# Reordering the turn from forward to backward in a one-core attention kernel: w3 before the rows of w4, q of the last head earlier, dq columns later

## The chip, the core and the metric

The kernel runs on one core of one Trainium2 chip. A core has a matrix engine (TensorE, PE in the profile), a vector engine (VectorE, DVE), an engine for functions of one element (ScalarE, ACT), GpSimd (POOL) and SyncE (SP), and 16 DMA engines that move data between HBM and the on-chip memories: SBUF, and PSUM, into which TensorE writes. Each engine takes its instructions in order. The metric is the device time of one execution in microseconds, as the median of several runs.

## The reference

One token passes through attention over a cache of 8192 keys and values in 32 heads of width 192, then through an MLP, both under adaptive layer norm. The reference returns the output and the gradients of nine inputs, the caches among them. Cut to what matters here (the mixer weights w1 and w2 and their inputs give no gradient that is returned, but w3 and w4 do):

```python
h = layernorm(x) * (1 + ca) + sa
q = (h @ wq).reshape(32, 192)
scores = einsum("hd,hkd->hk", q, k_cache) * 192 ** -0.5      # 8192 keys a head
o = einsum("hk,hkd->hd", softmax(scores), v_cache)
x = x + ga * (o.reshape(6144) @ wo)
h = layernorm(x) * (1 + cb) + sb
x1 = h                                                       # with one token the shifted mixer adds nothing
h2 = gelu(layernorm(x1) @ w3) @ w4                           # widths 640 -> 1536 -> 640
out = x + gb * (x1 + h2)
grads = vjp(out)(grad_out)       # d x, d k_cache, d v_cache, d wq, d wo, d w3, d w4, d c, d w_mod
```

The caches are 100 MB each and their gradients are as large, so the program reads and writes some 570 MB.

## The kernel before, in words

**Two loops and a turn between them.** The forward loop goes over heads 0 to 30 (`for i in range(H1)`). A head has K and V in two halves of 1536 KB, each 128 partitions by 32 keys by 192. For each head it forms the scores (VectorE products, summed by TensorE with the identity), the softmax, the weighted V (`vs`, four quarters a head, part on VectorE, part on ScalarE), and a matrix M = K^T (weighted V) with 193 columns, accumulated in the PSUM tile `mp` by `m_units`, from which dq is later made without reading K again. The backward loop goes over 64 half heads, last head first (`for s in range(NS)`): it reads a half of V, forms dP (products in `mul_q`, sums in `tree_q`, `dot_sum`), dS, the gradient of K (`dk_part`, VectorE: q times dS) and of V (`dv_groups`: TensorE outer products of a probability row and d(o), cast by ScalarE), and stores both through GpSimd's queue.

**The turn** lies between them and is a chain that nothing can be stored before: the last head's scores and output, the attention output, two layer norms, `n2_bf`, u = n2 @ w3 (`ups`, L831), gelu, d_g (eight or more calls in `dg_part`, VectorE sums of w4 rows times `dbo_bc`), du, dn = du @ w3^T (`dn_ps`, L926), and the gradient of the attention output `dao_bf` (L960). `w3t_gen` turns w3 by TensorE transposes in nine pieces, each copied out by ScalarE through two PSUM buffers; `w3t()` does the next piece. h2 = gelu(u) @ w4 (`h2_ps`) takes 60 matmuls of one column. `dw4_dve` and `dw4_act` form rows of the gradient of w4 in the place of the w4 rows in `qs_bc`. `do_mm(TL, b)` forms d(o) of one of the last two heads from `dao_bf`, and ScalarE writes it to `do_r`. After it come the first d(v) products, the trees of the first half head, and `q_bc(H1)`, which spreads the last head's q over the partitions for `dk_part`.

**What sets the order.** TensorE, VectorE, ScalarE and SyncE keep the order in which the program is written within each of two hand-ordered blocks (`manual_schedule`): the first ends with `d_sb_out`, the second begins after the backward pools are opened. Loads go on SyncE's queue in order: in the turn, the second half of V of the last head, w4 rows 0 to 3 with L660 into `w4b`, wo, rows 4 to 11 with L660 into `qs_bc` (called at L693), four fifths of w3 into `wp` (L695), the last fifth into `w3_4` (L704, named w in the profile), the V half for later (`v4`), the next wo, and the two probability rows `er_b` (L1002). A load is issued when its buffer is free: `wp` shares its buffer with the last score products. Stores go through GpSimd.

Pools of the forward part (`vs`, `ft`, the PSUM pools `psM`, `psO`, `psR`) end with the first block, and the backward pools (`bst` in SBUF, with `er_b`, `do_r`, `qh`; `psV`, `psR2`, `psT` in PSUM) take their space. `m_add` reads the tiles `mt` (pool `ft`) and `mp` (pool `psM`). For the last head q's dq has no M, so in half heads 0 and 1 `dq_rows` sums dS times K on TensorE and `dq_cols` turns the row into columns that VectorE adds.

The lines that wait for one another at the end of the first half heads, before the change:

```python
        if row is not None:
            dq_cols(row)
            row = None
        dk_part(dK, qh, dS4, 0, JQ)
```

Of the kernel before, what the change touches and what calls it, by code (L numbers as in the profile page):

```python
# [8 lines left out]
FP32 = mybir.dt.float32  # L9
# [11 lines left out]
def kernel(  # L21
# [27 lines left out]
    P = 128  # L49
# [55 lines left out]
    def pick(n, b):  # L105

        return ident_bf[0:n, b : b + 1].to_broadcast([n, P])
# [6 lines left out]
    def col(n, name, dtype=FP32):  # L114
        return const.tile([P, n], dtype, name=name)
# [5 lines left out]
    def mean_mm(src, n):  # L121
        ps = psS.tile([P, 32], FP32, name="mean_ps", tag="s")
        T_.matmul(ps[:, 0:n], lhsT=onesD, rhs=src, start=True, stop=True)
        return ps
# [235 lines left out]
    with tc.tile_pool(name="vs", bufs=3) as vsp, tc.tile_pool(name="ft", bufs=2) as ft, \  # L360
# [98 lines left out]
        def m_add(h, mp, mt):  # L459
            t, b = divmod(h, 2)  # L460
            V_.tensor_tensor(out=M2[64 * b : 64 * b + 64, t, :], in0=mp[0:64, MO : MO + MW], in1=mt[64:128, :], op=ALU.add)
# [49 lines left out]
        def dg_part(n):  # L511
            for a in dgs[:n]:
                V_.tensor_tensor_reduce(out=junk, in0=w4r(a), in1=dbo_bc, scale=1.0, scalar=0.0, op0=ALU.mult, op1=ALU.add, accum_out=d_g[:, a : a + 1])
            del dgs[:n]
# [3 lines left out]
        with tc.manual_schedule(engines=ORDER):  # L518
# [135 lines left out]
            def vs_act(vs, q, lo, hi):  # L654
                j0, v0 = q * JQ, (q % 2) * JQ
                for k in range(lo, hi):
                    A_.activation(out=vs[:, k, 0:DH], in_=vy[q // 2][:, v0 + k, :], func=ACT.Copy, scale=Ef[:, j0 + k : j0 + k + 1])

            def load_rows(dst, lo, hi):
                nc.sync.dma_start(out=dst.rearrange("p (a r) -> p a r", r=D), in_=w4v[:, lo:hi, :])  # L660
                for a in range(lo, hi):
                    w4rows[a] = dst[:, (a - lo) * D : (a - lo + 1) * D]
# [30 lines left out]
            load_rows(qs_bc[:, 0 : 8 * D], 4, 12)  # L693
# [10 lines left out]
            nc.sync.dma_start(out=w3_4, in_=w3d[:, 4, :])  # L704
            V_.tensor_copy(out=AO[:, :, 2 * TL - 2 : 2 * TL], in_=ps_ao)
# [37 lines left out]
            dg_part(1)  # L743
            V_.reciprocal(out=rinv[:, 2 * TL : 2 * TL + 2], in_=po[:, 4:6])
# [75 lines left out]
            def w3t(n=1):  # L820
                for _ in range(n):
                    next(w3t_it, None)

            w3t()
# [7 lines left out]
            m_add(H1 - 2, z["mp"], mt)  # L832
# [4 lines left out]
            vs_act(vs3, 3, 10, 14)  # L837
# [4 lines left out]
            A_.activation(out=w_, in_=w_, func=ACT.Exp, scale=-2.0 * GELU_K0)  # L842
            w3t()
# [12 lines left out]
            w3t()  # L856
            vs_act(vs3, 3, 14, JQ)
# [5 lines left out]
            pe.pop(0)()  # L863
            ps5 = mean_mm(sg.rearrange("p a b -> p (a b)"), 5 * ND)
# [20 lines left out]
            def dw4_dve(dst, a0, lo, hi):  # L885
                for a in range(lo, hi):
                    V_.tensor_scalar(out=dst[:, (a - a0) * D : (a - a0 + 1) * D], in0=dbo_bc, scalar1=g_[:, a : a + 1], scalar2=None, op0=ALU.mult)
# [25 lines left out]
            for k in range(ND):  # L913
                for a in range(NF):
                    T_.matmul(h2_ps[:, k : k + 1], lhsT=w4r(a)[:, k * P : (k + 1) * P], rhs=g_bf[:, a : a + 1], start=(a == 0), stop=(a == NF - 1))
# [12 lines left out]
            m_add(H1 - 1, mp, mt)  # L928
# [11 lines left out]
            V_.tensor_copy(out=bo, in_=h2_ps[:, 0:ND])  # L940
            dw4_dve(qs_bc, 0, 0, 3)
            pr = col(4 * ND, "pr").rearrange("p (a b) -> p a b", b=ND)
            V_.tensor_tensor(out=pr, in0=dn_ps[:, None, :].to_broadcast([P, 4, ND]), in1=G, op=ALU.mult)
            ps = mean_mm(pr.rearrange("p a b -> p (a b)"), 4 * ND)
# [5 lines left out]
            V_.scalar_tensor_tensor(out=B1, in0=vv, scalar=nr1, in1=dy_c, op0=ALU.mult, op1=ALU.add)  # L950
            d_n2, vg = col(ND, "d_n2"), col(ND, "vg")
            V_.tensor_tensor(out=vg, in0=Ag, in1=dn_ps, op=ALU.mult)
            V_.tensor_tensor(out=Bg, in0=B1, in1=ga, op=ALU.mult)
# [8 lines left out]
            dw4_dve(qs_bc, 0, 3, 6)  # L962
# [74 lines left out]

    do_mm(TL, 1)

# [36 lines left out]

    def q_bc(h):
        ps = psB.tile([P, 512], FP32, name="q_ps", tag="b")
        T_.matmul(ps[:, 0:DH], lhsT=pick(HQ, h), rhs=q_rows, start=True, stop=True)
        qh = bst.tile([P, DH], BF16, name="qh", bufs=2)  # L1080
        A_.copy(out=qh, in_=ps[:, 0:DH])
        return qh
# [241 lines left out]
    def dq_cols(row):  # L1324
        cp = psS.tile([P, 4], FP32, name="dq_c", tag="s")
        T_.matmul(cp[:, 0:1], lhsT=row[:, 0:P], rhs=c32[:, 0:1], start=True, stop=True)
        T_.matmul(cp[64:128, 1:2], lhsT=row[:, P:DH], rhs=c32[:, 0:1], start=True, stop=True)
        V_.tensor_tensor(out=dq_x[:, 2:3], in0=cp[:, 0:1], in1=dq_x[:, 2:3], op=ALU.add)
        V_.tensor_tensor(out=dq_x[64:128, 1:2], in0=cp[64:128, 1:2], in1=dq_x[64:128, 1:2], op=ALU.add)
# [44 lines left out]
    qh = q_bc(H1)  # L1374
    row = None
    late0 = [lambda: V_.scalar_tensor_tensor(out=du, in0=t_, scalar=-1.0, in1=d_g, op0=ALU.mult, op1=ALU.mult), dx1_out, d_sb_out]
    for s in range(NS):
# [47 lines left out]
        if row is not None:  # L1425
            dq_cols(row)
            row = None
# [10 lines left out]
        dk_store(s, dK, 0 if nxt else JQ, JH)  # L1438
        dv(5)
# [57 lines left out]
```

## Time and profile before

| | us |
|---|---|
| median of 3 runs | 1406.76 (1403.11 to 1409.83) |
| the profiled execution | 1405.93 |
| its span, first to last instruction | 1404.1 |
| TensorE busy | 1195.7 (85%) |
| VectorE busy | 1111.2 (79%) |
| ScalarE busy | 912.3 (65%) |
| transferred | 569.38 MB, mean 406 GB/s |

In the profile a line such as "L831" is a line of the kernel. "x60" counts instructions. A bracket at the end of a line of the timeline is the idle time of that engine before it and what ended it. The page cuts the span into 40 slices of 35.1 us; the granted clock of TensorE is given as a share of full speed. The times of the turn are counted in us from the start of the span.

### The profile page before, as it was taken

How to read it: one execution, taken by the hardware profiler on the slowest of the kernel's cores; microseconds unless marked ns; L12 is line 12 of the kernel's file. 1: busy time of each engine (PE TensorE's matmuls, PEld its weight loads, DVE VectorE, ACT ScalarE, POOL GpSimd, SP SyncE). 2: the span in 40 equal slices, each digit the busy share in tenths (PEclk: the TensorE clock that was granted, in tenths of full speed). 3: DMA queues.
4: the chain of work that ended last, by engine and by line, in shares of the span. 5: the costliest groups of instructions: out<-in, count | busy, mean ns of one | idle time of the engine just before them, and what ended most of it. 6: DMA issues, size and time to landing. Idle time of an engine off the chain costs nothing.

```text
span 1404.1 us, 30487 instructions
## 1 busy us (share of the span) xinstructions
PE 1195.7 (85%) x12712; PEld 748.7 (53%) x12712; DVE 1111.2 (79%) x1460; ACT 912.3 (65%) x2004; POOL 106.2 (8%) x192
## 2 busy tenths in 40 slices
PE   3999989999999998799866998698988987879985
PEld 2777777878777777543323444343443443334431
DVE  4999999999999997786765876776766767768775
ACT  0777777777777777566544766565656665556664
POOL 0000000000000000011110101101110101101110
PEclk9999999999999998755555555655555555555555
DMA  9999999999999997699999999999999999999998
GB/s 381 396 425 425 416 424 420 417 423 415 426 415 417 415 401 313 217 362 425 423 391 419 422 425 427 423 427 426 427 424 422 420 414 406 415 411 376 424 411 356
DMA packets 76232, 569.38 MB, mean 406 GB/s; under 512 B 7294, under 2 KB 25070, under 8 KB 36030
## 3 DMA queue, kind: packets, MB, share of 16 engines
q1 hardware_dynamic: 51146, 342.03, 59.5%
q0 software_dynamic: 24432, 224.89, 38.3%
q8 instruction: 99, 1.62, 0.4%
q10 hardware_dynamic: 516, 0.51, 0.1%
q14 instruction: 39, 0.32, 0.1%
HBM read 340.97 MB, written 226.44 MB: 404 GB/s over the span
## 4 chain that ended last, share of the span: by engine, by line
issue 48%; DVE 22%; DMA 11%; PE 9%; POOL 6%; ACT 2%; POOLq 0%; SPq 0%; ACTq 0%; DVEq 0%
DVE prod L333 9%; DMA KB<-in_A_k_cache_dram 8%; DVE prod L337 5%; DVE vs L383 3%; PE mp L405 3%; POOL out_dram L1337 2%; POOL out_dram L1333 2%; PE half_ps L343 2%; PE mp L410 1%; DMA out_dram<-VB 1%; DMA w<-in_B_w_dram 1%; DMA w_st<-in_A_wq_dram 1%; DVE pq L1044 1%; POOL out_dram L1176 1%; POOL out_dram L1203 1%
## 5 line engine op out<-in xcount | busy, mean ns | idle before, releaser
L1063 PE MATMUL dot_ps<-pq,ident_bf 128*128 128x256 bf16 x1494 | 384.4, 401 | 20.9 <-DVE dP L347 18.0
L390 ACT ACTIVATE vs<-VB,Ef 128x192 bf16<-128x192 bf16 x840 | 303.5, 447 | 0.0
L1075 ACT CAST KB<-dv_ps 128x768 bf16<-128x768 f32 x312 | 241.9, 803 | 78.2 <-PE dv_ps L1074 76.6
L1063 PEld LDWEIGHTS <-ident_bf 128*128 128x128 bf16 x1494 | 151.0, 124 | 178.6 <-issue 138.3
L1074 PE MATMUL dv_ps<-do_r,er_b 1*128 1x192 bf16 x2048 | 233.1, 341 | 3.0 <-ACT KB L1075 1.7
L333 DVE TENSOR_TENSOR prod<-KB,qs_bc 128x6144 bf16<-128x6144 bf16 x62 | 207.9, 3353 | 23.9 <-DMA KB<-in_A_k_cache_dram 16.2
L405 PE MATMUL mp<-vs,KB 128*128 128x193 bf16 x1984 | 190.2, 248 | 4.3 <-ACT vs L390 2.9
L1086 DVE TENSOR_TENSOR KB<-qh,dS 128x3072 bf16<-128x3072 bf16 x74 | 127.8, 1753 | 63.3 <-DMA out_dram<-KB 55.7
L405 PEld LDWEIGHTS <-KB 128*128 128x128 bf16 x1984 | 169.7, 98 | 13.4 <-DMA KB<-in_A_k_cache_dram 5.9
L902 ACT COPY wT<-wT_ps 128x1024 bf16<-128x1024 bf16 x82 | 79.1, 964 | 116.6 <-PE wT_ps L901 116.6
L1074 PEld LDWEIGHTS <-er_b 1*128 1x128 bf16 x2048 | 71.1, 105 | 148.7 <-issue 146.9
L343 PE MATMUL half_ps<-prod,ident_bf 128*128 128x256 bf16 x744 | 95.1, 279 | 43.2 <-DVE prod L337 43.1
L383 DVE TENSOR_TENSOR vs<-VB,E 128x1728 bf16<-128x1728 bf16 x120 | 123.7, 1052 | 0.3 <-ACT vs L390 0.3
L1044 DVE TENSOR_TENSOR pq<-VB,do_r 128x3072 bf16<-128x3072 bf16 x66 | 115.5, 1749 | 8.1 <-PE dot_ps L1063 8.1
L1044 DVE TENSOR_TENSOR pq<-KB,do_r 128x3072 bf16<-128x3072 bf16 x62 | 108.5, 1750 | 6.8 <-PE dot_ps L1063 6.2
L337 DVE TENSOR_TENSOR prod<-prod 128x3072 bf16<-128x3072 bf16 x62 | 108.7, 1754 | 1.0
L410 PE MATMUL mp<-vs,KB 128*64 128x193 bf16 x1976 | 107.5, 252 | 0.0
L343 PEld LDWEIGHTS <-ident_bf 128*128 128x128 bf16 x744 | 72.9, 99 | 61.5 <-issue 52.5
L1075 ACT CAST VB<-dv_ps 128x768 bf16<-128x768 f32 x96 | 75.1, 802 | 38.5 <-PE dv_ps L1074 38.3
L1075 ACT CAST qs_bc<-dv_ps 128x768 bf16<-128x768 f32 x104 | 80.6, 803 | 27.3 <-PE dv_ps L1074 26.9
L347 DVE TENSOR_REDUCE dP<-dot_ps 128x32 f32<-128x512 f32 x64 | 44.0, 688 | 62.6 <-PE dot_ps L1063 62.4
L410 PEld LDWEIGHTS <-KB 128*64 128x64 bf16 x1976 | 80.1, 110 | 19.9 <-issue 19.6
(369 smaller groups left out, 1191.7 us busy)
## 6 DMA issues: line engine op xcount, KB each, us to landing
VB<-in_A_v_cache_dram SPq DMA_DIRECT2D x93, 1536.0 KB
out_dram<-KB POOLq DMA_DIRECT2D x74, 1536.0 KB, 15.0
KB<-in_A_k_cache_dram SPq DMA_DIRECT2D x64, 1536.0 KB
KB<-in_A_v_cache_dram SPq DMA_DIRECT2D x31, 1536.0 KB
out_dram<-VB POOLq DMA_DIRECT2D x26, 1536.0 KB, 15.3
out_dram<-qs_bc POOLq DMA_DIRECT2D x25, 1536.0 KB, 14.4
wo_st<-in_A_wo_dram SPq DMA_DIRECT2D x31, 480.0 KB
w_st<-in_A_wq_dram SPq DMA_DIRECT2D x12, 960.0 KB
```

The lines of the kernel that those rows point to most:

```text
L333: V_.tensor_tensor(out=prod, in0=src, in1=vec[:, None, :].to_broadcast([P, JH, DH]), op=ALU.mult)
L337: V_.tensor_tensor(out=prod[:, :, 0:HW], in0=prod[:, :, 0:HW], in1=prod[:, :, DH - HW : DH], op=ALU.add)
L343: T_.matmul(ps, lhsT=ident_bf, rhs=prod[:, :, k : k + TF], start=(k == 0), stop=(k == w - TF))
L383: V_.tensor_tensor(out=vs[:, 0:n, 0:DH].rearrange("p j (a b) -> p j a b", b=4), in0=v[:, v0 : v0 + n, :].rearrange("p j (a b) -> p j a b", ...
L390: A_.activation(out=vs[:, k, 0:DH], in_=v[:, v0 + k, :], func=ACT.Copy, scale=Ef[:, j0 + k : j0 + k + 1])
L405: T_.matmul(mp[:, 0:MW], lhsT=kb[:, j0 + k, 0:P], rhs=vs[:, k, 0:MW], start=(q == 0 and k == 0), stop=(z and k == JQ - 1), skip_group_chec ...
L410: T_.matmul(mp[p0 : p0 + 64, MO : MO + MW], lhsT=kb[:, j0 + k, P:DH], rhs=vs[:, k, 0:MW], start=False, stop=(z and k >= JQ - 2), skip_grou ...
L1044: V_.tensor_tensor(out=pq[:, q], in0=v_l[s][:, q * JQ : (q + 1) * JQ, :], in1=do_of(ht(s)[0])[:, None, :].to_broadcast([P, JQ, DH]), op=AL ...
L1063: T_.matmul(ps[:, q * JQ : (q + 1) * JQ, :], lhsT=ident_bf, rhs=pq[:, q, :, k : k + TS], start=(k == 0), stop=(k == w - TS), skip_group_ch ...
L1074: T_.matmul(ps[:, b, k * DH : (k + 1) * DH], lhsT=er[p0 : p0 + 1, 2 * m + k, :], rhs=doh[p0 : p0 + 1, :], start=True, stop=True)
L1075: A_.copy(out=dV4[:, 2 * q : 2 * q + 2, m * PW : (m + 1) * PW], in_=ps[:, :, 0:PW])
L1086: V_.tensor_tensor(out=dK[:, lo:hi, :].rearrange("p j (a b) -> p j a b", b=4), in0=qh.rearrange("p (a b) -> p a b", b=4)[:, None, :, :].to ...
```

## The change

Three groups of moves; no operation is added or dropped, except that two of the six dw4 rows go from VectorE to ScalarE.

- In the turn's loads, rows 4 to 11 of w4 are issued after both parts of w3. On TensorE, the two main parts of M's third quarter (`m_units(2, ...)`) come before u without the piece of `w3t()` that stood ahead of them; two pieces of `w3t()` follow u, and the rest of M's third quarter is behind them. All of `vs3` is finished ahead of the Exp. `m_add` of head 30's predecessor goes ahead of the reciprocal of `po`. h2 is split: 36 matmuls before dn, 24 after the mean that follows dn. Small VectorE operations move ahead of `pr`; the dw4 rows, the copy of h2 and the `m_add` of M's last head move behind `dao_bf`.
- `q_bc(H1)` moves from just before the backward loop to between `do_mm(TL, 1)` and `do_mm(TL, 0)`, with its PSUM tile in `psS` in place of `psB`.
- In the loop, `dq_cols` moves behind `dk_part` and `dk_store`.

```diff
-            load_rows(qs_bc[:, 0 : 8 * D], 4, 12)
             wp = pp.tile([P, JH * DH], BF16, name="wp", tag="prod")
             nc.sync.dma_start(out=wp.rearrange("p (i n) -> p i n", i=4), in_=w3d[:, 0:4, :])
...
             nc.sync.dma_start(out=w3_4, in_=w3d[:, 4, :])
+            load_rows(qs_bc[:, 0 : 8 * D], 4, 12)
...
             dg_part(1)
+            m_add(H1 - 2, z["mp"], mt)
             V_.reciprocal(out=rinv[:, 2 * TL : 2 * TL + 2], in_=po[:, 4:6])
...
-            w3t()
             pe = m_units(2, ky[1], vs2, mp)
             pe.pop(0)()
             pe.pop(0)()
...
-            m_add(H1 - 2, z["mp"], mt)
             dg_part(1)
...
-            vs_act(vs3, 3, 10, 14)
+            vs_act(vs3, 3, 10, JQ)
...
             A_.activation(out=w_, in_=w_, func=ACT.Exp, scale=-2.0 * GELU_K0)
+            w3t()
             w3t()
...
-            w3t()
-            vs_act(vs3, 3, 14, JQ)
             pe.pop(0)()
             pe.pop(0)()
             w3t()
             w3t()
             pe = m_units(3, ky[1], vs3, mp)
             pe.pop(0)()
+            w3t()
...
-            for k in range(ND):
-                for a in range(NF):
-                    T_.matmul(h2_ps[:, k : k + 1], lhsT=w4r(a)[:, k * P : (k + 1) * P], rhs=g_bf[:, a : a + 1], start=(a == 0), stop=(a == NF - 1))
+
+            def h2_part(lo, hi):
+                for k in range(lo, hi):
+                    for a in range(NF):
+                        T_.matmul(h2_ps[:, k : k + 1], lhsT=w4r(a)[:, k * P : (k + 1) * P], rhs=g_bf[:, a : a + 1], start=(a == 0), stop=(a == NF - 1))
+
+            h2_part(0, 3)
...
-            m_add(H1 - 1, mp, mt)
...
-            V_.tensor_copy(out=bo, in_=h2_ps[:, 0:ND])
-            dw4_dve(qs_bc, 0, 0, 3)
-            pr = col(4 * ND, "pr").rearrange("p (a b) -> p a b", b=ND)
-            V_.tensor_tensor(out=pr, in0=dn_ps[:, None, :].to_broadcast([P, 4, ND]), in1=G, op=ALU.mult)
-            ps = mean_mm(pr.rearrange("p a b -> p (a b)"), 4 * ND)
             V_.tensor_scalar(out=A1, in0=cb1, scalar1=rho[:, 0:1], scalar2=None, op0=ALU.mult)
...
             V_.scalar_tensor_tensor(out=B1, in0=vv, scalar=nr1, in1=dy_c, op0=ALU.mult, op1=ALU.add)
+            V_.tensor_tensor(out=Bg, in0=B1, in1=ga, op=ALU.mult)
+            pr = col(4 * ND, "pr").rearrange("p (a b) -> p a b", b=ND)
+            V_.tensor_tensor(out=pr, in0=dn_ps[:, None, :].to_broadcast([P, 4, ND]), in1=G, op=ALU.mult)
+            ps = mean_mm(pr.rearrange("p a b -> p (a b)"), 4 * ND)
+            h2_part(3, ND)
+            dw4_act(qs_bc, 0, 0, 2)
...
             V_.tensor_copy(out=d_n2, in_=dn_ps)
-            dw4_dve(qs_bc, 0, 3, 6)
+            V_.tensor_copy(out=bo, in_=h2_ps[:, 0:ND])
+            dw4_dve(qs_bc, 0, 2, 6)
+            m_add(H1 - 1, mp, mt)
             dw4_store(qs_bc, 0, 6)
...
+    def q_bc(h, pool=psB, tag="b"):
+        ps = pool.tile([P, 2 * P], FP32, name="q_ps", tag=tag)
+        T_.matmul(ps[:, 0:DH], lhsT=pick(HQ, h), rhs=q_rows, start=True, stop=True)
+        qh = bst.tile([P, DH], BF16, name="qh", bufs=2)
+        A_.copy(out=qh, in_=ps[:, 0:DH])
+        return qh
+
     do_mm(TL, 1)
+    qh = q_bc(H1, psS, "s")
...
-    qh = q_bc(H1)
     row = None
...
-        if row is not None:
-            dq_cols(row)
-            row = None
         dk_part(dK, qh, dS4, 0, JQ)
...
         dk_store(s, dK, 0 if nxt else JQ, JH)
+        if row is not None:
+            dq_cols(row)
+            row = None
         dv(5)
```

More of the change, by code (lines that the diff above doesn't have):

```diff
@@ L950 @@
             V_.scalar_tensor_tensor(out=B1, in0=vv, scalar=nr1, in1=dy_c, op0=ALU.mult, op1=ALU.add)
+            V_.tensor_tensor(out=Bg, in0=B1, in1=ga, op=ALU.mult)
[4 more added lines that the diff above has]
+            dw4_act(qs_bc, 0, 0, 2)
             d_n2, vg = col(ND, "d_n2"), col(ND, "vg")
             V_.tensor_tensor(out=vg, in0=Ag, in1=dn_ps, op=ALU.mult)
-            V_.tensor_tensor(out=Bg, in0=B1, in1=ga, op=ALU.mult)
             V_.tensor_tensor(out=vg, in0=vg, in1=Bg, op=ALU.add)
@@ L1075, in dv_groups @@
             A_.copy(out=dV4[:, 2 * q : 2 * q + 2, m * PW : (m + 1) * PW], in_=ps[:, :, 0:PW])
[L1077 to L1082, printed above, removed]
     def dk_part(dK, qh, dS4, lo, hi):
```

## The prediction

> **What bounds the kernel now.** I read the page's slices first, to see which stage wastes the transfers.
>
> ```profile
> span 1404.1 us, 30487 instructions
> DMA  9999999999999997699999999999999999999998
> GB/s 381 396 425 425 416 424 420 417 423 415 426 415 417 415 401 313 217 362 425 423 391 419 422 425 427 423 427 426 427 424 422 420 414 406 415 411 376 424 411 356
> ```
>
> A slice is 35.1 us. The transfers run at about 420 GB/s nearly everywhere, so both big loops are bound by bytes. The hole is in slices 15 to 17 (527 to 632 us), between the last forward head and the start of the backward loop. Stretches of that hole (window, then busy us of each engine, granted clock, DMA share, GB/s):
>
> ```profile
> 554.00:556.00 2.00, 2.00 (x28) 1.89 (x27) 0.00 (x0) 1.56 (x5) 0.00 (x0) 0.50 0.10 43
> 558.00:560.00 2.00, 2.00 (x23) 1.53 (x22) 1.93 (x14) 1.95 (x6) 0.33 (x1) 0.50 0.00 0
> 568.00:572.00 4.00, 2.19 (x40) 1.70 (x38) 3.41 (x21) 0.95 (x2) 0.00 (x0) 0.78 0.04 10
> 588.00:592.00 4.00, 0.00 (x0) 0.00 (x0) 4.00 (x4) 1.22 (x2) 0.54 (x1) 0.84 0.81 338
> 600.00:604.00 4.00, 4.00 (x49) 2.24 (x51) 3.03 (x5) 2.45 (x4) 1.07 (x2) 0.50 0.58 246
> 604.00:608.00 4.00, 3.28 (x42) 1.77 (x34) 1.86 (x2) 3.08 (x7) 0.00 (x0) 0.95 0.99 408
> ```
>
> From 554 to 572 us nothing moves, because every buffer waits for arithmetic; up to 604 the transfers still have dips; from 604 they are full. So what the arithmetic gains before 604 shortens the run, as long as there is a dip to fill. The chain of waits (start, us, what) says which arithmetic:
>
> ```profile
> 539.38 13.09 DMA w<-in_B_w_dram
> 553.13 2.59 PE mp L405 x16
> 555.71 1.58 PE u_ps L831 x60
> 568.86 0.18 DVE pr L943
> 570.62 0.18 DVE dao_bf L960
> 586.31 0.21 ACT qh L1081
> ```
>
> TensorE waits 13 us for w3, then does the third quarter of M and u, then everything up to dn. In the timeline, the lines that set the new order:
>
> ```profile
> 549.99 0.23 DVE L797 TENSOR_SCALAR n_bf<-hx,r 128x5 bf16<-128x5 f32 x1 [0.19 <-ACT r L151]
> 552.52 0.29 PE L814 MATMUL w3T_ps<-ident_bf,w 128*128 128x128 bf16 x1 [0.32 <-DMA w<-in_B_w_dram]
> 566.40 0.35 DVE L461 TENSOR_TENSOR M<-mp,mt 64x193 f32<-64x193 f32 x1
> 568.75 1.12 SPq L1002 DMA_DIRECT2D er_b<-eT_d  x2
> 586.54 3.43 DVE L1086 TENSOR_TENSOR VB<-qh,dS 128x3072 bf16<-128x3072 bf16 x2 [3.48 <-ACT qh L1081]
> 609.00 0.16 DVE L1328 TENSOR_TENSOR dq_x<-dq_c,dq_x 128x1 f32<-128x1 f32 x1 [3.13 <-PE dq_c L1327]
> ```
>
> To be seen: n2 is ready at 550.2, w3 lands at 552.5; VectorE waits 3.48 us for q before the first dK and 3.13 us for the dq columns before a later one; and SyncE issues the two er loads, the first transfers of the backward loop, only at 568.75.
>
> **The change, part by part.** The sum is made against the profiled execution: 1404.1 us span, 1405.93 us in all, 0.8 us under the median of 1406.76.
>
> *Load order.* The 8 rows of w4 (1280 KB) go behind w3 on SyncE's queue. Between 540 and 548 the queue moves 385 to 407 GB/s, so 1.31 MB less in front is 3.3 us: w3 lands near 549.2 in place of 552.5. SyncE issues the load of wp (L695) at 538.14 as before, since the buffer becomes free then. The earlier loads (v, w4b, wo) still run till about 541.3, counted back in bytes, so the queue does not run dry by more than half a microsecond. The rows are then issued at about 541 instead of 531.95 and land at about 552.5, where w3 did. The first row of them is wanted by the d_g products, in the new order at about 555.5: nothing, with 3 us of cover. The v4 load behind keeps its place (issue 548.83).
>
> *M of the third quarter ahead of u.* Before: w3 at 552.5, a w3 transposition, M (2.59 us), u at 555.50. After: TensorE is free at 549.1 (end of the er transposes L465), M's 16 matmuls take 549.1 to 551.75 at the half clock granted then, and u starts at 551.75, with n2 (550.2) and w3 (549.2) both there. Gain 3.75 us. Bounds: 2.95 if w3 still lands at 552.5; 4.85 if M runs at full clock (1.5 us, as the 16 matmuls at 527.80 do). I take 3.75, as the clock at 546 to 556 is 0.50 in every stretch.
>
> *From u to dn.* The two transpositions go behind u, M's rest behind them; ScalarE gets one 1.01 us copy behind the Exp and loses two vs products (0.83). VectorE's chain is untouched: u, gelu, then eight d_g rows of 0.865 us; du is ready 3.75 us earlier. TensorE does 36 of 60 h2 matmuls before dn rather than 60: 0.6 us less, and dn could start 0.8 us earlier before it met du (566.37 in the old time). I take 0.6; bounds 0 and 0.8. m_add of the third-last M slips into the 0.51 us in which VectorE waits for po: nothing; 0.35 if that gap closes.
>
> *From dn to dao.* Five small VectorE operations and three dw4 rows now stand ahead of pr; the mean is read at once and not 0.4 us late. The rest of h2 (0.6 us) runs while VectorE makes dao: nothing. So dao_bf is ready 3.75 + 0.6 + 0.4 = 4.75 us earlier, at about 566.
>
> *What this adds.* Behind dao_bf VectorE has now d_n2, bo, four dw4 rows (0.323 each, from 0.97 for three) and the m_add of the last M (0.35): it ends at about 567.7. Before, that m_add ran at 566.40, long ahead of need. SyncE's own waits show that the er loads waited first for it (1.1 us), then for dn (2.0 us): the backward buffers lie where the forward pools were. So they now start at 567.7, only 1.05 us earlier. What is queued behind: SyncE's next load, not due till later; do_r on ScalarE (do_ps ready at 567.1, so 0.7 us late, and past two dw4 rows of 0.74 us that end by 567.2); and all of TensorE behind the first dv products, which need er. Small loads land in 1.7 us at best (the er row written from vs) and 4.7 us for the 960 KB store issued in the same moment; the er load of before took under 3.0 (568.75 to 571.75). I take 2.5, nearest to that bound with the store beside it: dv starts at 570.3, 2.0 us earlier than 572.33. TensorE had 0.62 + 0.25 us of waiting in its next products, which goes. dP of the first half head: 2.9 us earlier (bounds 0.7 for 4.7 us, 3.7 for 1.7).
>
> *q early.* q's matmul and copy (0.3 us each) now stand beside the d(o) products, where ScalarE and TensorE wait for er anyhow: nothing, or 0.3. VectorE's wait of 3.48 us goes, since the multiply before it ends at 583.06 and q is there. What is late next: the six dw4 rows on ScalarE (4.42 us) end about when the second dP is due, 0.1 us of slack. Gain 3.35, bounds 2.4 and 3.48.
>
> *dq columns behind dK.* The two dK run 2.7 and 3.1 us earlier and their stores with them, but in these steps dP waits for TensorE (0.93 us at 603.12), whose work is the same: the gain there is the two waits of TensorE for VectorE (0.43 and 0.42), of which I take half, 0.4. Bounds 0 and 0.9.
>
> **Sum:** 2.9 + 3.35 + 0.4 = 6.65 us ahead at the point where the transfers fill up. The dips to be filled: 18 us empty up to 572, 7.2 us idle share from 572 to 604, 4.0 of these after 584. So the lead fits, and 1405.93 - 6.65 = 1399.3 us.
>
> **Rivals.**
>
> *The transfers take part of it.* After 584 only the dips at 588 to 592 (0.76 us) and 600 to 604 (1.68 us) are filled, the rest being mixed reads and writes: 2.9 + 2.4 = 5.3, 1400.6 us, or 1402 if q's gain is all that is capped. For it: share 0.99 from 604 on; against: only 246 GB/s at 600.
>
> *Better.* The clock opens during M (1.1 us), er lands in 1.7 us (0.8), the earlier stores fill 1 us more: 1396.4 us. For it: TensorE has no gap before M now; against: clock 0.50 there.
>
> *The clock stays halved up to dn.* In the trace it opens at about 560, after TensorE had been busy without a break from 552.5, and stays 1.00 to 568, where w3's transposes share TensorE with M. If the transposes just behind u held it back, all after u would run at half clock: 60 transposes at 0.108 (1.30 for 12), M at 2.6 and twice 1.4, h2 and dn 2.5, do's transposes 1.6, mean 0.2, in all 16.3 us from 553.4, dn ends at 569.7 in place of 564.4, 5.3 us lost: 1404.6 us. The Trainium skill speaks for it: "TensorE: Matmul & The Clock Gate", Part 4, says that transposes do not count as work for the gate. By that rule the time would be the 1404.6 of this case; the trace agrees only in part, since the clock was 1.00 while transposes were a third of TensorE's work.
>
> *Slower: er lands late.* With the lead at 7.5 us for an er load that costs no delay and 1 us less for each us that it lands after 1.65 us, the gain is gone at a landing of 9.2 us. Landings in the full stretches are 12.9 us (a 1.2 KB store) and 17.3 (the wo store): 1409.7 and 1414.1 us. Against it: the queues are empty at 568 to 572 (share 0.04).
>
> *The order of loads does nothing* (w3 waits for another transfer) and the er delay stays: 0.8 us less, 1400.1; with u's operands late by the 1.3 MB after all and q capped, 1404.
>
> **How the numbers follow.** About 0.5% (7.0 us) is what a measurement can tell here from no change; faster by that means below 1399.7, on which the forecast lies. Forecast, 1397 to 1401.5: 0.48, with 0.31 of it below 1399.7. Better: 0.12, all faster. Transfers: 0.14; clock: 0.06; order: 0.07, all within 0.5%. Late er: 0.13, 0.07 of it slower by over 0.5%. Faster 0.43, within 0.50, slower 0.07. The range 1395 to 1405 leaves out the late er beyond 8 us and the far end of better.
>
> **What would show it.** u at about 551.7 with no wait for w3; M just ahead of it; d_g rows without a wait for w4; the two er loads right behind the last m_add, near 567.7, and the first dv products waiting for them, not for do_r; the first dK with no wait for q, near 579; no wait for dq columns ahead of dK; the clock at 1.00 from 557 on. I am wrong if the empty stretch up to the first store does not shrink by 3 us or more, or if the share of the transfers from 580 to 604 stays under 0.85.

## The result

The changed kernel takes 1399.44 us (median of 8 runs) against 1406.63 us of the kernel before (8 runs): a ratio of 0.9943, 95% interval 0.9924 to 0.9962. (The ratio is taken over all runs; the two medians alone give 0.9949, or 7.2 us.) A second comparison, with other runs of both kernels, gave 0.9932 (0.9912 to 0.9951). The profiled execution took 1397.46 us; its span was 1395.7 us, against 1404.1 before.

The slices of the profile of the kernel after (40 slices, now of 34.9 us; DMA in tenths):

```profile
span 1395.7 us, 30490 instructions
DMA  9999999999999998699999999999999999999998
GB/s 382 397 423 426 421 421 420 418 418 421 426 417 416 407 409 344 234 418 428 422 396 407 425 425 427 423 423 423 427 419 425 419 417 412 411 402 382 422 410 356
```

The hole is one slice narrower: the third of its slices (362 GB/s before) now runs at 418. Stretches of it in the kernel after (window, busy us of PE, PEld, DVE, ACT and POOL, granted clock, DMA share, GB/s):

```profile
550.00:552.00 2.00, 2.00 (x58) 1.80 (x55) 1.77 (x8) 1.97 (x7) 0.00 (x0) 1.00 0.91 238
558.00:560.00 2.00, 1.99 (x33) 1.49 (x31) 1.93 (x5) 1.79 (x3) 0.00 (x0) 1.00 0.04 8
568.00:572.00 4.00, 2.89 (x22) 1.51 (x24) 3.93 (x4) 2.35 (x4) 0.00 (x0) 0.50 0.70 252
580.00:584.00 4.00, 2.11 (x50) 1.53 (x49) 4.00 (x4) 3.75 (x6) 1.38 (x2) 1.00 0.51 212
588.00:592.00 4.00, 3.40 (x62) 2.18 (x62) 3.94 (x7) 3.99 (x7) 0.53 (x1) 1.00 1.05 341
600.00:604.00 4.00, 2.70 (x16) 1.17 (x15) 3.93 (x7) 2.53 (x5) 1.08 (x2) 0.54 0.99 423
```

To be seen: transfers move at 568 to 572 (share 0.70, before 0.04); the dips at 588 and 600 are gone (1.05 and 0.99, before 0.81 and 0.58); and the clock is 1.00 at 550 and at 588, where it was 0.50 and falling. One dip is new: at 580 to 584 the share is 0.51, where it was 0.92. Added up over stretches of 4 us from 548 to 620 us (the part of each share that is missing from 1.00, times 4 us), the transfers' idle time falls from 24.1 to 16.4 us: from 16.3 to 13.4 up to 572, from 3.2 to 2.8 up to 584, and from 4.6 to 0.24 behind that. These 7.7 us agree with the gain, 7.2 us by the medians and 8.0 by the ratio.

The timeline of the kernel after, in the order in which the prediction went through it:

```profile
549.34 1.51 PE L405 MATMUL mp<-vs,KB 128*128 128x193 bf16 x16
550.47 0.23 DVE L798 TENSOR_SCALAR n_bf<-hx,r 128x5 bf16<-128x5 f32 x1 [0.20 <-ACT r L151]
550.85 0.24 PE L831 MATMUL u_ps<-n_bf,wp 128*128 128x1 bf16 x4
552.35 0.38 PE L815 MATMUL w3T_ps<-ident_bf,wp 128*128 128x128 bf16 x4
565.01 0.17 DVE L962 TENSOR_TENSOR dao_bf<-vg,qr 128x5 bf16<-128x5 f32 x1
566.52 0.35 DVE L461 TENSOR_TENSOR M<-mp,mt 64x193 f32<-64x193 f32 x1
566.94 1.12 SPq L1006 DMA_DIRECT2D er_b<-eT_d  x2
569.11 0.82 PE L1086 MATMUL dv_ps<-do_r,er_b 1*128 1x192 bf16 x8 [2.97 <-DMA er_b<-eT_d]
578.69 3.42 DVE L1091 TENSOR_TENSOR VB<-qh,dS 128x3072 bf16<-128x3072 bf16 x2
598.86 0.15 DVE L1333 TENSOR_TENSOR dq_x<-dq_c,dq_x 128x1 f32<-128x1 f32 x1
608.39 3.43 DVE L1091 TENSOR_TENSOR qs_bc<-qh,dS 128x3072 bf16<-128x3072 bf16 x2 [3.75 <-issue]
619.39 3.43 DVE L1091 TENSOR_TENSOR KB<-qh,dS 128x3072 bf16<-128x3072 bf16 x2 [2.18 <-DMA out_dram<-KB]
```

M's third quarter takes 1.51 us before u, which waits for no load; the er loads are issued right behind the last `m_add`, and the first d(v) products wait for them; the first dK (578.69) has no wait for q, and the dq columns (598.86) no wait for TensorE. The last two lines are new: VectorE waits ahead of 608 for something that the profile does not name, and ahead of 619 for a store that must leave its buffer. At least there the arithmetic has run ahead of the transfers.

How far ahead, by the start of `dP` in each half head (us from the span's start, from the timelines):

| dP of half head | 0 | 1 | 2 | 3 |
|---|---|---|---|---|
| before | 580.32 | 591.55 | 603.12 | 615.47 |
| after | 576.03 | 583.69 | 591.89 | 601.01 |
| earlier by | 4.3 | 7.9 | 11.2 | 14.5 |

The arithmetic is 14.5 us ahead by the fourth half head and the run is 7 to 10 us shorter. The lead is over twice the 6.65 us of the forecast's sum, while the time agrees with it within the interval; the difference between the two is what the experiments had to explain.

### The profile page after: what moved, and what is told of

Its sections match the earlier page's. It is cut to its first block, busy times and chain, and to the rows that moved or that the text cites. A ratio compares the mean times of both kernels' runs of the same rounds, so it can differ in the third digit from the quotient of the medians.

```text
span 1395.7 us, 30490 instructions
## 1 busy us (share of the span) xinstructions
PE 1171.3 (84%) x12712; PEld 738.4 (53%) x12712; DVE 1110.2 (80%) x1458; ACT 910.9 (65%) x2006; POOL 106.0 (8%) x192
## 4 chain that ended last, share of the span: by engine, by line
issue 47%; DVE 23%; DMA 13%; PE 9%; POOL 5%; ACT 1%; POOLq 0%; SPq 0%; DVEq 0%
DVE prod L333 10%; DMA KB<-in_A_k_cache_dram 9%; DVE prod L337 5%; DVE vs L383 3%; PE mp L405 2%; POOL out_dram L1342 2%; POOL out_dram L1338 2%; PE half_ps L343 2%; PE mp L410 1%; DMA out_dram<-VB 1%; DMA out_dram<-wo_st 1%; PE dot_ps L1075 1%; DMA wo_st<-in_A_wo_dram 1%; POOL out_dram L1181 1%; DVE S_h L347 1%
## 5 line engine op out<-in xcount | busy, mean ns | idle before, releaser
L1075 PE MATMUL dot_ps<-pq,ident_bf 128*128 128x256 bf16 x1494 | 371.0, 389 | 23.7 <-DVE dP L347 21.4
L1075 PEld LDWEIGHTS <-ident_bf 128*128 128x128 bf16 x1494 | 147.6, 122 | 174.1 <-issue 137.0
L1086 PE MATMUL dv_ps<-do_r,er_b 1*128 1x192 bf16 x2048 | 228.1, 332 | 6.6 <-DMA er_b<-eT_d 3.0
L405 PEld LDWEIGHTS <-KB 128*128 128x128 bf16 x1984 | 168.9, 97 | 13.1 <-issue 4.6
L343 PEld LDWEIGHTS <-ident_bf 128*128 128x128 bf16 x744 | 72.9, 100 | 61.8 <-issue 52.9
L370 ACT ACTIVATE E<-S_h,negm 128x256 bf16<-128x256 f32 x31 | 15.8, 508 | 114.2 <-DVE negm L541 111.9
## 6 DMA issues: line engine op xcount, KB each, us to landing
out_dram<-KB POOLq DMA_DIRECT2D x74, 1536.0 KB, 16.2
out_dram<-VB POOLq DMA_DIRECT2D x26, 1536.0 KB, 15.3
```

The source lines that it names most:

```text
L343: T_.matmul(ps, lhsT=ident_bf, rhs=prod[:, :, k : k + TF], start=(k == 0), stop=(k == w - TF))
L405: T_.matmul(mp[:, 0:MW], lhsT=kb[:, j0 + k, 0:P], rhs=vs[:, k, 0:MW], start=(q == 0 and k == 0), stop=(z and k == JQ - 1), skip_group_chec ...
L1075: T_.matmul(ps[:, q * JQ : (q + 1) * JQ, :], lhsT=ident_bf, rhs=pq[:, q, :, k : k + TS], start=(k == 0), stop=(k == w - TS), skip_group_ch ...
L1086: T_.matmul(ps[:, b, k * DH : (k + 1) * DH], lhsT=er[p0 : p0 + 1, 2 * m + k, :], rhs=doh[p0 : p0 + 1, :], start=True, stop=True)
```

## The experiments

Twelve runs followed, of eleven kernels (the changed kernel itself among them), on three chips. The table gives each with its ratio to the kernel before on the same chip; "gain" is that ratio's distance from 1 times about 1406.6 us; "idle" is the transfers' idle time from 548 to 620 us, added up as above; "dP 0 to 3" is the time from the first dP to the fourth; "pause" is TensorE's longest wait for `dP` between the first half heads, in 580 to 593 us.

| kernel | ratio (95% interval) | gain, us | idle, us | dP 0 to 3, us | pause, us |
|---|---|---|---|---|---|
| before | 1 | 0 | 24.1 | 35.2 | 4.61 |
| after | 0.9943 (0.9924 to 0.9962) | 8.0 | 16.4 | 25.0 | 2.31 |
| after, again | 0.9932 (0.9912 to 0.9951) | 9.6 | 15.3 | 25.0 | 2.03 |
| after, dq columns in front | 0.9935 (0.9911 to 0.9960) | 9.1 | 16.5 | 27.0 | 2.05 |
| after, q late | 0.9968 (0.9951 to 0.9984) | 4.5 | 19.0 | 35.2 | 4.61 |
| after, rows of w4 first | 0.9938 (0.9916 to 0.9959) | 8.7 | 17.1 | 26.0 | 1.34 |
| after, m_add early | 0.9926 (0.9900 to 0.9952) | 10.4 | 14.6 | 29.9 | 2.42 |
| after, m_add early, again | 0.9948 (0.9929 to 0.9966) | 7.3 | 15.0 | 25.0 | 2.26 |
| after, delay late | 0.9951 (0.9933 to 0.9969) | 6.9 | 16.2 | 25.0 | 2.25 |
| after, delay early | 0.9976 (0.9961 to 0.9991) | 3.4 | 21.7 | 25.0 | 2.05 |
| before, turn alone | 0.9996 (0.9980 to 1.0011) | 0.6 | 21.8 | 37.8 | 4.60 |
| before, q alone | 0.9965 (0.9951 to 0.9979) | 4.9 | 19.4 | 27.0 | 2.28 |
| before, turn and q | 0.9936 (0.9912 to 0.9960) | 9.0 | 15.6 | 27.0 | 2.24 |
| before, turn and dq columns | 0.9954 (0.9936 to 0.9971) | 6.5 | 16.8 | 30.2 | 4.51 |

A single profile scatters by up to 5.3 us in where the turn begins (the operation that makes n2 starts between 548.34 and 553.67 us in these runs), so the verdicts rest on the ratios, and the profiles serve for durations inside them.

Two columns belong together. In all thirteen rows below the first, the drop of the idle time from 24.1 us is within 1.8 us of the gain, though one comes from a single profile and the other from all runs. The lead does not go with the gain in this way: a way of 25.0 us from the first dP to the fourth stands beside gains from 3.4 to 9.6 us, and one of 29.9 beside 10.4.

### The changed kernel, dq columns back in front of dK

```diff
+        if row is not None:
+            dq_cols(row)
+            row = None
         dk_part(dK, qh, dS4, 0, JQ)
...
         dk_store(s, dK, 0 if nxt else JQ, JH)
-        if row is not None:
-            dq_cols(row)
-            row = None
```

> The changed kernel with the dq columns back in front of the first half of dK; everything else as changed. Theory A (only transfer idle time counts: the 16 DMA engines stood idle 24.1 us between 548 and 620 before and 16.4 us after, and after 584 only 0.2 us are left, so lead of the arithmetic beyond that is swallowed): the waits for the columns return, dP of half head 3 comes 2 to 5 us later than 601.0, the idle time after 584 grows by at most 1 us, and the time stays within 1 us of the changed kernel's 1399.4. Theory B (the lead of the arithmetic carries to the end): the time grows by the 3 us and more that the chain loses, 1402 to 1404.

Measured 0.9935 (1397.53 us), no loss against the changed kernel's 0.9943 and 0.9932, although the way from the first dP to the fourth is 2.0 us longer (27.0 against 25.0). The dq columns behind dK speed up the arithmetic by more than the 0.4 us of the prediction, and the run doesn't notice: with q early the arithmetic is far enough ahead. The first theory holds on the time; the idle time behind 584 us grew somewhat more than it allowed (from 0.24 to 1.9 us).

### The changed kernel, q as late as before

```diff
     do_mm(TL, 1)
-    qh = q_bc(H1, psS, "s")
...
     V_.memset(dsc, 0.0)
+    qh = q_bc(H1)
     row = None
```

> The changed kernel with q of the last head spread only after the six dw4 rows, as before. Theory A: the first dK waits 3.5 us again, its store slips behind by as much, the dip of the transfers at 580 to 584 (2.0 us idle) grows by 2 to 3 us, and the time is 1401.5 to 1402.5. Theory B: the full 3.4 us and the open clock after it are lost, 1403 or more. A third reading, that the wait was hidden anyway: 1399.4.

Measured 0.9968 (1402.18 us, in the range of the first theory): 3.5 us of the changed kernel's gain are lost by its first comparison, 5.1 by its second. The whole of the arithmetic's gain between the half heads goes as well: from the first dP to the fourth it takes 35.2 us again, as before. So q is worth much more to the chain than its 3.48 us of waiting; in the time, a loss of 3.5 to 5.1 us can't be told from these 3.48.

### The changed kernel, rows of w4 loaded ahead of w3 as before

```diff
             score_tree(1, d1)
+            load_rows(qs_bc[:, 0 : 8 * D], 4, 12)
             wp = pp.tile([P, JH * DH], BF16, name="wp", tag="prod")
...
             nc.sync.dma_start(out=w3_4, in_=w3d[:, 4, :])
-            load_rows(qs_bc[:, 0 : 8 * D], 4, 12)
```

> The changed kernel with rows 4 to 11 of w4 loaded before w3 again; M of the third quarter stays ahead of u. Theory A: w3 lands at 552.5 and u starts at about 552.6 in place of 550.9; every step up to the first store is 1.7 us later and so is the end, 1401.1; if TensorE's clock falls in the wait, the transposes and M behind u cost 2 us more, 1403. Rival (the order of loads gives nothing, the gain of u is all from M): 1399.4, u at 550.9.

Measured 0.9938: no loss. In the timeline of this kernel the last part of w3 still came in only just behind u's first operands:

```profile
548.76 0.24 PE L831 MATMUL u_ps<-n_bf,wp 128*128 128x1 bf16 x4 [0.81 <-DVE n_bf L798]
549.43 0.18 PE L831 MATMUL u_ps<-n_bf,w 128*128 128x1 bf16 x1 [0.43 <-DMA w<-in_B_w_dram]
551.02 0.17 DVE L838 COPY u<-u_ps 128x12 f32<-128x12 f32 x1 [0.60 <-PE u_ps L831]
```

From n2 to u's copy it took 2.63 us against 2.05 in the changed kernel. So the order of the loads is worth some 0.6 us in this profile, not the 1.7 us that was expected, and none of it shows in the time; what moved u was mainly the order on TensorE. (The last part of w3 landed 11.4 us after its issue here, 13.1 in the kernel before, so another run may pay more.)

### The changed kernel, the last m_add early again

```diff
+            m_add(H1 - 1, mp, mt)
             sk = mean_sum(ps5, 5, "sk")
...
             dw4_dve(qs_bc, 0, 2, 6)
-            m_add(H1 - 1, mp, mt)
```

> The changed kernel with the m_add of the last M back ahead of the NW chain, where it stood before; nothing else moves. Theory A: the two er loads, which in the changed kernel leave 0.1 us after that m_add (566.94), leave right behind dn at 563.7, land by 565.8, and the first dv products wait for do_r alone, 567.0 in place of 569.1; the transfers start their stores 2 us earlier and the time falls by 1.7 to 2.2 us, to 1397.5. Rival (the lead is already more than the transfers can use): the first dv products come 2 us earlier and the time stays 1399.4.

In its timeline the er loads are issued at dn's end and not behind `dao_bf`, and the d(v) products wait only for d(o):

```profile
561.82 0.35 DVE L461 TENSOR_TENSOR M<-mp,mt 64x193 f32<-64x193 f32 x1 [0.22 <-ACT mt L449]
563.63 1.12 SPq L1006 DMA_DIRECT2D er_b<-eT_d  x2
567.17 0.82 PE L1086 MATMUL dv_ps<-do_r,er_b 1*128 1x192 bf16 x8 [0.24 <-ACT do_r L1032]
```

So the cost that the prediction put on the moved `m_add` is there: the first transfers of the backward pools wait for the last reader of the forward pools. In time it gave 0.9926, ahead of the changed kernel but within its interval. It was run a second time:

> The changed kernel with the last m_add put back ahead of the mean behind dn, a second time, to see whether it is faster than the changed kernel (0.9932 and 0.9943 in two comparisons, 0.9926 for this one). Theory A (the backward pools' first transfers wait for it; 1.8 us less idle before 620 us): 0.9915 to 0.9930. Rival (the transfers are full from 580 us on, an er load earlier is worth nothing): the changed kernel's own 0.9930 to 0.9945.

Measured 0.9948. The two together can't be told from the changed kernel's two; if the early `m_add` is worth anything, it is under what 6 to 8 runs resolve. The first d(v) products start 1.9 us sooner (567.17 against 569.11), the first dP only 0.9 us (575.17 against 576.03).

### Extra work late and early in the changed kernel

Two kernels do extra work whose results change nothing: the first repeats one product of 1.75 us three times in the fourth half head, the second repeats six of the d_g sums ahead of du. A run of the changed kernel stood beside them.

```diff
             mul_q(s + 1, 1)
+            if s == 3:
+                for _ in range(3):
+                    mul_q(s + 1, 1)
```

> The changed kernel with 5.25 us of VectorE work put into half head 3, behind its dP: the product for the next half head's second quarter is formed four times in place of once (three more of 1.75 us). Theory A (from about 584 on the transfers are full and the lead of the arithmetic beyond some 8 us is swallowed; dP of half head 3 was 14.5 us earlier than before the change while the run ended only 7.2 us earlier): the time stays within 1.5 us of the changed kernel, at most 1401. Theory B (each us of the chain counts to the end): 5.25 us more, 1404.7.

```diff
             dg_part(NF)
+            for a in range(4, 10):
+                V_.tensor_tensor_reduce(out=junk, in0=w4r(a), in1=dbo_bc, ..., accum_out=d_g[:, a : a + 1])
```

> The changed kernel with 5.2 us of VectorE work put ahead of du: six of the d_g sums are formed twice (0.865 us each). Theory A (while the transfers stand empty each us of the chain counts): dn, dao and the first store 5.2 us later, the empty time 5.2 us longer, the time 5.2 us more, 1404.6. A rival by which the lead at the first store is more than the transfers can use: less than 2 us more.

> The changed kernel itself, as the measure for the delays beside it: 1399.4, as in its first runs.

On the same chip the changed kernel took 1397.36 us, the one with 5.25 us of work late 1398.95, the one with 5.2 us early 1403.18. Late, 1.6 us of 5.25 were paid by the medians and 2.7 by the ratios, and the transfers' idle time rose by 1.0 us; early, 5.8 us (6.2 by the ratios), with 6.4 us more idle time. The cost of the late work is known to 2 us at best; that it is less than that of the early work is clear. In its timeline it stands where VectorE had waited 3.82 us in the run beside it, and from the fourth dP to the fifth it took 14.99 us in place of 13.54. So work costs about what it adds to the idle time of the transfers: by the fourth half head most of it is swallowed by the lead, ahead of du none of it.

### The kernel before with the turn alone

The turn's first half on the kernel before: w3 ahead of the rows of w4, M's third quarter ahead of u, the w3 pieces behind it; q, the dq columns and everything behind dn stay. (Edits of `vs_act`, of `m_add(H1 - 2)` and of the other `w3t()` calls, as in the change, are left out here.)

```diff
-            load_rows(qs_bc[:, 0 : 8 * D], 4, 12)
...
             nc.sync.dma_start(out=w3_4, in_=w3d[:, 4, :])
+            load_rows(qs_bc[:, 0 : 8 * D], 4, 12)
...
-            w3t()
             pe = m_units(2, ky[1], vs2, mp)
...
+            w3t()
             w3t()
```

> The kernel before with only the first part of the turn changed: w3 ahead of the w4 rows, M of the third quarter ahead of u, two pieces of w3's transposition behind u, the third vs quarter finished ahead of the Exp, the m_add of head 29 earlier. The tail (h2 whole ahead of dn, m_add of the last M early, dw4 rows), q and the dq columns are as before. Theory A: n2 to u is 0.4 us in place of 5.5, dn and, since the er loads wait for dn only, the first dv products come 4.5 to 5 us earlier; q's wait of 3.5 us stays: 1401.5 to 1402.5. Rival (the gain is q's and the dq columns'): 1405 or more.

No gain: 0.9996, as the rival had it. Yet the first d(v) product stood at 566.28 us, 6.0 us earlier than before, of which 1.0 was there already at n2 (548.98 against 549.99). Where the lead went, in this kernel's stretches and timeline:

```profile
584.00:588.00 4.00, 1.76 (x10) 0.81 (x10) 3.96 (x4) 0.27 (x1) 0.54 (x1) 0.57 0.78 331
592.00:596.00 4.00, 4.00 (x28) 1.97 (x28) 4.00 (x4) 3.30 (x5) 0.53 (x1) 0.50 0.51 215
604.00:608.00 4.00, 3.57 (x23) 1.98 (x22) 2.33 (x5) 1.60 (x2) 0.00 (x0) 0.50 0.94 384
608.00:612.00 4.00, 4.00 (x30) 1.77 (x30) 3.90 (x8) 3.10 (x5) 0.62 (x2) 0.50 0.25 104
```

```profile
580.50 3.43 DVE L1085 TENSOR_TENSOR VB<-qh,dS 128x3072 bf16<-128x3072 bf16 x2 [3.48 <-ACT qh L1080]
586.24 1.01 PE L1062 MATMUL dot_ps<-pq,ident_bf 128*128 128x256 bf16 x4 [4.60 <-DVE dP L347]
605.60 0.16 DVE L1327 TENSOR_TENSOR dq_x<-dq_c,dq_x 128x1 f32<-128x1 f32 x1 [5.79 <-PE dq_c L1326]
```

VectorE waits 3.48 us for q; TensorE, which has nothing to do meanwhile, pauses 4.60 us; its clock goes to 0.50 and stays there past 612 us (before, it was back at 0.95 and 0.90 from 604 to 612); so the TensorE work of the half heads takes longer, and VectorE waits 5.79 us for the dq columns, in place of 3.13. The lead of 6 us at the first dP is 3.4 us at the fourth (612.07 against 615.47), and the transfers stand at a share of 0.25 from 608 to 612. This one profiled run was still 2.4 us faster than the profiled run of before; over 12 runs the ratio shows 0.6 us, and the median is 0.3 us above that of before on the same chip.

### Which part lets the lead through

Three kernels put q, or the dq columns, to work without the rest. The edits are those shown above, on the kernel before: q spread early alone; q early and the turn; the dq columns behind dK and the turn.

> The kernel before with q spread early and nothing else. Prediction's term: the 3.48 us wait ahead of the first dK goes, 3.35 us gained (2.4 to 3.48), ratio 0.9975 to 0.9983. Theory A (a gain counts as far as the transfers have idle time behind it; 4.6 us of idle share lie after 584 us): 2 to 3.4 us, ratio 0.9976 to 0.9986. Theory E (VectorE then waits as much longer for the dq columns or for buffers): under 1 us, ratio over 0.9993.

> The kernel before with the turn alone (w3 ahead of the w4 rows, M's third quarter ahead of u) gained nothing (ratio 0.9996), although its first dv stood 6 us earlier. Here q is spread early as well; dq columns and everything behind dn stay as before. Theory A (VectorE is what gives the lead back: 3.5 us of waiting for q and 5.8 us for the dq columns ahead of dK; with q early its lead is large enough that the first dK starts 5 to 8 us earlier and the stores with it): ratio 0.9935 to 0.9965, 5 to 9 us gained, transfers' idle share after 584 us under 2 us. Theory B (the parts add up, and the turn is worth nothing by itself): q's 3.4 us or less, ratio 0.9976 to 0.999. Theory C (the dq columns are what holds): no gain, ratio 0.9985 to 1.0005, with VectorE waiting 5 us or more for them.

> The turn alone on the kernel before, with the dq columns behind dK as well; q stays late. Theory C (the 5.8 us wait for the dq columns was where the turn's lead went): the wait goes, ratio 0.9960 to 0.9980, 3 to 5.5 us gained. Theory B (terms add up; dq columns are worth 0.4 us): ratio 0.9985 to 1.0005. Theory D (the lead goes to TensorE's clock in the first half heads, which stood at 0.50 in that run from 584 to 616 us): no gain either if the clock is at 0.50 there again, 4 us if it is open.

q alone gives 4.9 us (3.0 to 6.9), more than any of the three expectations, though the interval takes in the 3.48 us of its wait. With the turn on top it gives 9.0 us, as much as the whole change: dq columns, the moved `m_add` and the order behind dn add nothing that could be measured. The turn with the dq columns gives 6.5 us, the turn alone 0.6. So the turn is worth nothing by itself that could be measured (0.6 us, -1.5 to 2.8) and some 4 us beside q (9.0 less 4.9, on the same chip; the two intervals overlap by a little); what it is worth beside the dq columns is not shown, since these were not run alone. Of the theories, the first (VectorE is what gives the lead back) holds for the turn with q; for the turn with the dq columns the expected 3 to 5.5 us are reached and passed. The theory that the prediction's terms add up missed both ratios; that the measured parts don't add up (0.6 and 4.9 against 9.0) is likely, but the intervals don't prove it.

The theory of the clock, for the turn with the dq columns, is not out either. In that profile the clock was 0.50 only from 586 to 592 us and then 0.84 and 1.00; with the turn alone it stayed at 0.50 past 612. Whether the 5.9 us between these two kernels come from the dq columns or from the clock, these runs don't separate.

Why q is worth more to the chain than its wait is seen in the kernel with q alone, in the stretches that answer to those of before from 588 to 604 us:

```profile
588.00:592.00 4.00, 1.72 (x21) 0.95 (x18) 3.96 (x5) 2.34 (x4) 1.38 (x2) 1.00 0.77 304
592.00:596.00 4.00, 4.00 (x48) 2.78 (x48) 3.39 (x5) 3.37 (x6) 0.00 (x0) 1.00 1.12 399
600.00:604.00 4.00, 3.58 (x37) 2.01 (x36) 2.76 (x4) 3.00 (x6) 0.00 (x0) 1.00 0.99 414
```

The same kind of stretches in the kernel before:

```profile
588.00:592.00 4.00, 0.00 (x0) 0.00 (x0) 4.00 (x4) 1.22 (x2) 0.54 (x1) 0.84 0.81 338
592.00:596.00 4.00, 3.71 (x22) 1.84 (x21) 2.26 (x3) 1.60 (x2) 0.00 (x0) 0.50 0.97 347
596.00:600.00 4.00, 4.00 (x30) 2.51 (x30) 3.31 (x4) 2.37 (x3) 0.00 (x0) 0.50 0.88 347
```

Before, TensorE does nothing from 588 to 592, and comes back at a clock of 0.50: 22 matmuls in 3.71 us. With q early its pause is 2.28 us, the clock stays at 1.00, and it does 48 matmuls in 4 us. In the table, all four kernels with q late have a pause of 4.5 to 4.6 us and a clock of 0.50 behind it, for some 4 us in one and 12 us or more in three; in eight of the ten rows with q early (pauses of 2.0 to 2.3 us) the clock stays at 1.00 for the next 14 to 16 us. (Then it falls in all eight without such a pause; why, no run here shows.) The Trainium skill, "TensorE: Matmul & The Clock Gate", Part 1, states a rule for such pauses: after an idle window of about 3.4 us the clock is halved. The pauses of 4.5 us agree with it. Two profiles don't fit it so neatly: where the rows of w4 were loaded first the clock was at 0.50 for a moment behind a pause of 1.34 us (584 to 586), and with the `m_add` early, the first time, from 586 to 598 us behind one of 2.42 us. In that last one the fourth dP came 4 us later than in the changed kernel, and the transfers were full from 584 us all the same (0.16 us idle).

The two profiles of the kernel with the `m_add` early show, as far as two profiles can, what the clock alone does, since the program is the same. From 588 to 592 us, the first time and again:

```profile
588.00:592.00 4.00, 4.00 (x29) 2.19 (x29) 2.97 (x5) 2.86 (x5) 0.53 (x1) 0.50 1.07 326
588.00:592.00 4.00, 3.12 (x50) 1.81 (x38) 3.93 (x5) 3.67 (x9) 0.53 (x1) 1.00 0.98 299
```

From the first dP to the second both took 7.66 us; from the first to the fourth 29.9 with the clock at 0.50 and 25.0 with it at 1.00. That is 4.9 us of the chain, about what q early gave beyond its wait (8.2 less 3.57).

## Why the prediction was right

The time was 1399.3 us on record and came out at 1399.4. That they meet to 0.1 us is luck: the sum got there by two errors that offset each other. It put the lead at less than half of what it became, and it took all of the lead as gain, where only part of it was; the second it had named as a rival.

**Load order.** It cost nothing, as said: u found w3 there, and the d_g rows found theirs. That it would bring w3 some 3 us earlier is not borne out: with the rows first, u waited only 0.43 us for it. The prediction also read a row of the chain wrongly. The 13.09 us there are the load of w3 from issue to landing, and not a wait of TensorE, which in the kernel before stood still for w3 for 2.47 us and then 0.32:

```profile
551.60 0.61 PE L814 MATMUL w3T_ps<-ident_bf,wp 128*128 128x128 bf16 x4 [2.47 <-DMA wp<-in_B_w_dram]
```

**M ahead of u.** u came 4.65 us earlier against 3.75 forecast, with n2 0.5 us later than in the profile of before. The bound of 4.85 us for a full clock was the true one: M's 16 matmuls took 1.51 us, and the clock was 0.72 at 548 to 550 and 1.00 from 550 on. Taking the clock from the windows of before failed, most likely because in these TensorE had a pause ahead of M, waiting for w3 (busy 1.13 and 0.41 of each 2 us from 548 to 552), and now it had none (2.00 of each 2).

**From u to dao.** du came 4.8 us earlier, dn 5.2, `dao_bf` 5.6. Beyond the 4.65 of u and 0.2 up to du these are 0.4 from du to dn, where h2's split acts (0.6 forecast), and 0.4 from dn to `dao_bf` (0.4).

**The m_add and the er loads.** The step held: VectorE ended the last `m_add` at 566.9, SyncE issued the er loads at that moment, and TensorE waited for them 2.97 us. They landed 2.03 us after their issue against 2.5 taken, so the first d(v) product came 3.2 us earlier (2.0 forecast), and the first dP 4.3 us (2.9). Undone, this cost gave a timeline with d(v) 1.9 us sooner and no time that could be measured.

**q early.** This is the term that was mis-sized. The wait of 3.48 us went, and the second dP was 3.57 us further ahead, as the 3.35 us had it. But the term stopped at VectorE. q's wait was also a pause of TensorE, and what the pause did to the clock was left out: with q alone moved, the way from the first dP to the fourth fell by 8.2 us (35.2 to 27.0). The row of 588 to 592 with 0.00 us of TensorE, and that of 600 to 604 with a clock of 0.50, were on show in the prediction's own fence, and read only as dips of the transfers.

**dq columns.** 0.4 us forecast, 2.0 in the chain when put back, none in the time once q is early. With q late, 5.9 us lie between the turn with them and the turn alone, with the clock as a rival cause.

**"So the lead fits."** This step failed. The lead was 14.5 us at the fourth half head and not 6.65, and only about 8 of it shortened the run; the dips behind 572 us could fill 3.2 + 4.6 us and are now down to 2.8 + 0.24. What the forecast put down as a rival, that the transfers take part of the lead, is what acts, on a lead twice as large. The delay put in late shows it: 1.6 to 2.7 us paid of 5.25.

**The other rivals.** The case of the clock halved up to dn did not come about: the transposes directly behind u (552.35) ran at 1.00, five of them in 0.27 us by their starts (552.35 to 552.62), and the clock stayed at 1.00 up to 564. The Trainium skill's rule that transposes don't count for the gate ("TensorE: Matmul & The Clock Gate", Part 4) would have led to that case. In this trace transposes ran at the full clock and did not close it, but the clock was open before them and matmuls lay between them, so transposes by themselves are not tested. The late er load didn't come about either (2.03 us). The "better" case was right in the clock during M; its er load in 1.7 us came only part of the way (2.03).

**Its signs of being wrong.** One was a share of the transfers under 0.85 from 580 to 604; it was 0.93 (0.82 before). The other was an empty stretch up to the first store that shrinks by less than 3 us: the transfers start for good at 568 us in place of 573, but the idle time up to 572 fell only from 16.3 to 13.4, so by the first count this sign stayed away, and by the second it came by 0.1 us.

**What stays open.** Why the turn alone gains nothing rests on one profile in which the clock stayed low behind q's pause; that it always does, with q late, in that kernel, was not tried. In the changed kernel without its early q, which has the dq columns behind dK as well, the lead does come through in part (4.5 us). And what the turn's order saves varies: with the turn as before, u came 5.51 us behind the start of n2's operation in the profile of before, but 3.14 in that of the kernel with q alone, where w3 kept TensorE waiting less (1.10 and 0.53 us); in all kernels with the new order it was 0.37 to 0.57.

## What to carry to other kernels

Where a stage ends in a part that is bound by transfers, price each edit by the idle time of the transfers that it removes and not by its place in the chain; past the point where they are full, a longer lead bought nothing here that could be measured, and an added 5.25 us cost 1.6 to 2.7. When an engine's wait goes, look at who else stood still in it: behind pauses of TensorE of 4.5 us its clock was at 0.50 for 12 us or more in three profiles of four, and that cost the chain more than the wait itself. And don't add up parts that were priced alone: here 0.6 and 4.9 made 9.0 (with wide intervals), and the whole change made no more than those two.

## What the runs showed beyond what was expected

- The clock opened during M, most likely because TensorE no longer paused ahead of it: 16 matmuls of 193 columns took 1.51 us, where 2.6 were forecast from the stretches of before.
- Four pauses of TensorE of 4.5 to 4.6 us were each followed by a clock of 0.50; pauses of 2.0 to 2.3 us left it at 1.00 in eight profiles.
- Two loads of 8 KB, issued while nothing moved, were there 2.03 us after their issue, beside a store of 960 KB.
- By 608 to 619 us the changed kernel's VectorE waits (3.75 us, which the profile puts down to no engine, and 2.18 us for a store) while the transfers are full: the turn has stopped being the bound there, and most of what is left to gain lies ahead of 572 us, where 13.4 us of transfer time are still empty.
